# Banded and causal attention on one Trainium2 core: one ring of eight PSUM banks, results of two rows, rows 0 and 1 as one piece, triangles cut in SBUF, engines from a table, and a new order

## The chip, the core and the metric

The kernel runs on one core of one Trainium2 chip. The metric is device time in microseconds for one launch, the median of several runs. The engines are TensorE (PE; its weight loads PEld), VectorE (DVE), ScalarE (ACT), GpSimd (POOL) and SyncE (SP), whose queue issues every DMA of this kernel.

## What is computed

Two layers in a row, all in float32, for 4 batches and 768 positions. First, banded attention with sinks: 8 heads of 64, each position sees its own 128 last positions and the first 4 (the sinks). Its output, 512 wide, is the input of the second layer: 4 experts, each one head of causal attention, with the two best experts of each position kept and weighed.

```python
# first layer, scale = 1/8
keep = is_sink | ((rel >= 0) & (rel < 128))          # rel = query - key
a = softmax(where(keep, scale * q @ k.T, -1e9));  x = a @ v
# second layer
logits = x @ w_gate;  w = softmax over the top 2 of 4
for e in range(4):
    q, k, v = x @ wq[e], x @ wk[e], x @ wv[e]
    a = softmax(where(causal, -1e9, scale * q @ k.T))
    out += (w of e, where chosen) * (a @ v @ wo[e])
```

## The kernel before

**The work.** A unit of the first layer (`first`, `band_rows`) is one batch and a pair of heads: 16 units. One of the second layer (`second`, `wide_rows`) is one batch and a pair of experts: 8 units. A row is a block of 128 positions; each has six. A unit turns q and k around (transposes on PE through an identity for batch 0, on DVE for the others), multiplies them to scores, takes the minimum and the exponential, scales by the reciprocal sum, transposes the probabilities and multiplies them with the values. The second layer also projects x to q, k and v (`second`, `values`) and stores (`store`). Some rows of the second layer send their probabilities through DRAM and back in place of the transposes (`by_way_of_dram`: POOL scales, DVE transposes in blocks, SP sends `there` and back).

**In the first layer**, rows 0 and 1 are done each for itself (`edge_row`), rows 2 and 3 and rows 4 and 5 as bands of two (`both_rows`, `transposed_band`). A band takes 132 keys per query, since the upper triangle of the row's own block and the lower triangle of the block before fill one 128 wide block (`pick`). After the transposes, PSUM is copied to SBUF (`pt`), and a second copy, multiplied by the triangle `own`, is taken from PSUM by DVE (`tri`, line 1471); the weighted sum (`av`) uses both, one with the values and one with the differences of neighbouring values (`dv`).

**On PE** matmuls use the array in three shapes, which the profile prints as rows*columns: 64*128, two heads beside each other in the rows (scores, transposes, the sums over the sinks in line 1393); 128*64, two heads beside each other in the columns (weighted sums, line 1389); 128*128 (projections, gate, output). PSUM has eight banks: six tiles `b` for everything and two tiles `acc` for the weighted sums of up to four rows (`Acc`), which ACT and DVE then split into a high and a low part (`finisher`, `split`, lines 1228 and 1233).

**The order.** Every piece of work is a `Step` with a priority, the engines that can do it, a cost for each, and the buffers it needs. `Plan.emit` runs through time: of all steps that can go, it takes on each engine the one with the best priority, start time and shape of the array, with `HURRY`, `STAY` and `BULK` as weights, and `NUDGE` adds a number to the priority of single steps. The steps are then issued in that order. While PE would be idle in the first part, `fill` puts dummy products there (lines 1059 and 1062). Steps that two engines can do (copies from PSUM, `evacuate`) go to the one that is free first. Buffers of a kind form a ring and are waited for.

**Weights** come on SP's queue, wv and the gate, wq, wk and wo, through the tiles `v2` and `o`; ACT rounds them to the high part and POOL takes the difference as the low part (`weight`, lines 1186 and 1190).

Of the kernel before, what the change touches and what calls it, by code (L numbers as in the profile page):

```python
# [34 lines left out]
PSUM = ("b", "acc")  # L35

NUDGE = {
    "busy_PE": -21.445, " ": -65.5699, " busy_PE": 26.9069, " busy_PE 0": 94.2732, "sink_values_DVE": -57.9649,
    " sink_values_DVE": -0.2231, " sink_values_DVE 0": -114.2035, "load_SP": 1.3276, " load_SP": 86.4402,
    " load_SP 0": -217.458, "again_SP": -58.9971, " again_SP 0": -60.4741, "sink_values_ACT": 63.7817,  # L40
    " sink_values_ACT": 11.9388, " sink_values_ACT 0": -13.5634, "sink_values_POOL": 86.9205, " sink_values_POOL": -18.6515,
    " sink_values_POOL 0": -126.024, "sink_values_SP": 5.8101, " sink_values_SP 0": 30.073, " load_SP 1": 1.7522,
    "weight_ACT": 29.2113, " weight_ACT": 38.9392, " weight_ACT 0": 363.4815, "weight_POOL": 62.3002,
    " weight_POOL": -88.56, " weight_POOL 0": 327.5217, " weight_ACT 1": 373.0797, " weight_POOL 1": 63.7488,
# [1896 lines left out]
```

## Time and profile before

| | |
|---|---|
| median of 3 runs | 383.38 us (382.5 to 384.05) |
| profiled execution | 383.73 us, span 381.7 us |
| PE busy | 373.7 us (98%), 4116 matmul records |
| weight loads busy | 314.7 us (82%) |
| DVE, ACT, POOL busy | 317.9 (83%), 253.7 (66%), 230.2 (60%) us |
| moved by DMA | 48.06 MB, mean 126 GB/s |

The span goes from the first to the last instruction of the profiled execution. Busy times of PE include the time in which one matmul follows another late without a gap being drawn, so its share alone doesn't say how dense PE's work is; the starts of neighbouring blocks of matmuls do.

### The profile page before, as it was taken

The page shows a single profiled execution, that of the slowest core. Times are in us where ns is not written, and L with a number is a line of the kernel's source. Part 1 is how long each engine was busy: PE and PEld are TensorE (multiplying, and loading weights), DVE is VectorE, ACT ScalarE, POOL GpSimd, SP SyncE. Part 2 cuts the span into 40 slices and gives each one's busy share as a digit, 9 for nine tenths or more (in the row PEclk, how much of TensorE's full clock was granted, in tenths as well). Part 3 has the DMA queues.
Part 4 walks back from the last instruction along what each step waited for, and adds up shares of the span by engine and source line. Part 5 has one row for each costly group of instructions (what it writes and reads, how often), then busy time and mean ns, then how long its engine had stood idle before and what let it go on. Part 6 is the DMA issues. An engine that isn't in the chain of part 4 may idle for free.

```text
span 381.7 us, 12237 instructions
## 1 busy us (share of the span) xinstructions
PE 373.7 (98%) x4116; PEld 314.7 (82%) x4116; DVE 317.9 (83%) x1420; ACT 253.7 (66%) x923; POOL 230.2 (60%) x429
## 2 busy tenths in 40 slices
PE   8999999999998999999999999999999999999996
PEld 7777787988787888988888788988788888988884
DVE  7999999599998999969699999657999858447952
ACT  3898997267897578738498767514899847215921
POOL 5789997548676853356478845059187830049830
PEclk9999999999999999999999999999999999999999
DMA  7989999435676877148665894037700000012004
GB/s 161 198 188 167 180 184 179 67 61 166 198 158 160 230 179 146 23 122 283 199 141 90 224 252 102 0 113 256 234 23 3 2 2 3 29 56 84 4 2 165
DMA packets 145631, 48.06 MB, mean 126 GB/s; under 512 B 122976, under 2 KB 138336, under 8 KB 145568
## 3 DMA queue, kind: packets, MB, share of 16 engines
q1 hardware_dynamic: 145568, 47.28, 50.9%
q8 instruction: 32, 0.52, 0.6%
q14 instruction: 31, 0.25, 0.2%
HBM read 30.88 MB, written 16.12 MB: 123 GB/s over the span
## 4 chain that ended last, share of the span: by engine, by line
PE 90%; DVE 5%; DMA 1%; SPq 1%; issue 1%; ACT 0%; POOL 0%; DVEq 0%; POOLq 0%
PE acc L1389 20%; PE b L1759 18%; PE b L1358 11%; PE b L1416 10%; PE b L1786 9%; PE b L1833 9%; PE b L1363 9%; PE acc L1393 2%; PE b L1844 1%; DMA kn<-in_k_dram 1%; SPq L1507 1%; DVE p L1663 1%; DVE b L1660 1%; DMA p<-there 1%; SPq L1727 0%
## 5 line engine op out<-in xcount | busy, mean ns | idle before, releaser
L1566 ACT ACTIVATE p<-p,st 128x768 f32<-128x768 f32 (+5 forms) x96 | 63.9, 668 | 14.9 <-DVE st L1558 14.0
L1245 ACT ACTIVATE pt<-b 128x256 f32<-128x256 f32 (+2 forms) x153 | 52.0, 372 | 9.6 <-PE b L1416 8.7
L1358 PE MATMUL b<-kx,qn 64*128 64x260 f32 (+1 forms) x384 | 57.2, 390 | 0.4 <-ACT qn L1245 0.3
L1667 ACT ACTIVATE p<-p,st 128x132 f32<-128x132 f32 x128 | 50.8, 399 | 8.4 <-DVE st L1663 6.9
L1578 POOL TENSOR_TENSOR p<-p,st 128x128 f32<-128x128 f32 (+5 forms) x66 | 50.4, 787 | 1.2 <-PE b L1416 0.2
L1558 DVE CUSTOM_DVE_ANT_0 p<-b,cmask 128x384 f32<-128x384 f32 (+3 forms) x96 | 45.7, 504 | 2.9 <-PE b L1363 2.3
L1363 PE MATMUL b<-ks,qs 64*128 64x384 f32 (+3 forms) x384 | 43.5, 342 | 0.0
L1416 PE MATMUL b<-ident,p 64*128 64x64 f32 x820 | 43.2, 228 | 0.2 <-ACT kx L1245 0.2
L1641 POOL TENSOR_TENSOR p<-p,st 128x256 f32<-128x256 f32 (+1 forms) x32 | 26.6, 833 | 27.1 <-DVE st L1405 6.4
L1358 PEld LDWEIGHTS b<-kx,qn 64*128 64x128 f32 x384 | 36.6, 186 | 7.5 <-DVE st L1663 1.5
L1416 PEld LDWEIGHTS b<-ident,p 64*128 64x128 f32 x820 | 34.6, 138 | 8.8 <-issue 4.0
L1389 PE MATMUL acc<-pt,vn 128*64 128x128 f32 x448 | 40.0, 282 | 0.2
L1502 POOL TENSOR_TENSOR p<-p,st 128x640 f32<-128x640 f32 (+2 forms) x30 | 37.3, 1254 | 0.8 <-POOL st L1408 0.3
L1786 PE MATMUL b<-wvh,x 128*128 128x260 f32 x192 | 37.1, 284 | 0.0
L1363 PEld LDWEIGHTS b<-ks,qs 64*128 64x128 f32 x384 | 31.5, 186 | 3.8 <-issue 1.8
L1833 PE MATMUL b<-woh,y 128*128 128x512 f32 x96 | 33.7, 399 | 0.0
L1663 DVE CUSTOM_DVE_ANT_0 p<-b,pair_mask 128x132 f32<-128x132 f32 x128 | 33.5, 284 | 0.0
L1686 POOL TENSOR_TENSOR p<-p,st 128x512 f32<-128x512 f32 x32 | 33.1, 1041 | 0.0
L1759 PE MATMUL b<-x,wqh 128*128 128x512 f32 (+1 forms) x128 | 33.0, 343 | 0.0
L1660 DVE COPY_PREDICATED b<-earlier,b 128x128 f32<-128x128 int32 x128 | 32.3, 286 | 0.8 <-PE b L1358 0.8
L1759 PE MATMUL b<-x,wkh 128*128 128x512 f32 (+1 forms) x128 | 32.9, 343 | 0.0
L1808 POOL TENSOR_TENSOR gate<-gate 128x24 f32<-128x24 f32 x4 | 0.9, 237 | 51.8 <-DVE gate L1803 51.8
(131 smaller groups left out, 979.1 us busy)
## 6 DMA issues: line engine op xcount, KB each, us to landing
vn<-in_v_dram SPq DMA_DIRECT2D x32, 192.0 KB, 3.5
out_dram<-o SPq DMA_DIRECT2D x24, 256.0 KB, 2.0
qn<-in_q_dram SPq DMA_DIRECT2D x52, 96.0 KB, 2.5
kn<-in_k_dram SPq DMA_DIRECT2D x52, 96.0 KB, 2.5
there<-p SPq DMA_DIRECT2D x10, 384.0 KB, 3.0
p<-there SPq DMA_DIRECT2D x40, 96.0 KB, 3.3
there<-p SPq DMA_DIRECT2D x10, 320.0 KB, 2.2
p<-there SPq DMA_DIRECT2D x40, 80.0 KB, 2.3
```

The costliest lines, as they stand in the source:

```text
L1245: nc.scalar.activation(dst(), src(), AF.Copy)
L1358: nc.tensor.matmul(o, self.q_of()[hs, qs], self.ks.t[hs, 0, ks], start=True, stop=True)
L1363: nc.tensor.matmul(o, self.qs.t[hs, a, qs], self.ks.t[hs, b, ks], start=n == 0, stop=n == 2)
L1389: nc.tensor.matmul(o[e * 64:e * 64 + 64], lhs, rhs, start=e not in self.begun, stop=last and self.done == len(self.steps))
L1416: nc.tensor.transpose(t[g].t[:, n, :], x[gs], ident[gs, gs])
L1558: nc.vector.tensor_tensor_reduce(out=one(e)[:, cs], in0=s2[e].t[:, :(c1 - c0) * 128], in1=mask(c0, c1), scale=times, scalar=st.t[:, 3, es] ...
L1566: nc.scalar.activation(x, x, AF.Exp, bias=st.t[:, 0, es], scale=-1.0, accum_out=st.t[:, 1, es])
L1578: nc.gpsimd.tensor_mul(x, x, st.t[:, 2, e:e + 1].to_broadcast([128, n * 128]))
L1667: nc.scalar.activation(p.t[:, n, :], p.t[:, n, :], AF.Exp, bias=st.t[:, 0, n:n + 1], scale=-1.0, accum_out=st.t[:, 1, n:n + 1])
L1759: nc.tensor.matmul(t.t, w[a][:, c, es], X[b, c].t[:, x, cs], start=c == 0 and m == 0, stop=c == NCH - 1 and m == 2)
L1786: nc.tensor.matmul(t.t[:, :VW], X[b, c].t[:, a, qs], W["wv"][w][:, c, :], start=c == 0 and n == 0, stop=c == NCH - 1 and n == 2)
L1833: nc.tensor.matmul(t.t, Y[b, c].t[:, a, qs], W["wo"][w][:, c, :], start=c == 0 and n == 0, stop=c == EP - 1 and n == 2)
```

## The change

- `PSUM` and `kinds`: the two `acc` tiles go, and `b` has eight tiles; a weighted sum takes a bank of the same ring. Results are finished in groups of two rows (`ROWS = "0 2 4 6"`); projections keep groups of four and two (`CUTS`).
- `edge_rows` in place of `edge_row`: rows 0 and 1 have one pair of score tiles (128 and 256 columns, without the sink columns), one set of sums and reciprocals, one block of 12 transposes and one weighted sum.
- `transposed_band`: the triangle is cut from the copy in SBUF, after both copies, in one instruction of 512 columns on POOL or DVE; the weighted sum waits for it too.
- `ONLY`, a table of steps and engines: it sets which engine does a step that two can do. New such steps are the scalings (`scaled`: POOL or ACT; a band's: POOL or DVE), the low parts of the weights (`either`), the differences of values and the triangle.
- wq and wk go through the tiles `o` in two pieces each.
- `NUDGE`, `HURRY`, `STAY` and `BULK` have other numbers: the order of all engines is new.

```diff
-PSUM = ("b", "acc")
+PSUM = ("b",)
 NUDGE = {
-    "busy_PE": -21.445, " ": -65.5699, " busy_PE": 26.9069, " busy_PE 0": 94.2732, "sink_values_DVE": -57.9649,
+    "busy_PE": -150.4, " ": -5.3, " busy_PE 0": 186.9, "sink_values_DVE": -89.8, " sink_values_DVE": -42.0,
...
+ONLY = {
+    " low_POOLDVE 0": DVE, " low_POOLDVE 1": POOL, " low_POOLDVE 2": POOL, " low_POOLDVE 5": POOL, " low_POOLDVE 6": POOL,
...
-HURRY = 37.208573
-STAY = 45.808617
-BULK = -17.350682
+HURRY = 55.95
+STAY = 129.39
+BULK = -27.41
...
             s.prio += sum(NUDGE.get(name, 0.0) for name in s.part)
+            if s.part[-1] in ONLY:
+                s.cost = {ONLY[s.part[-1]]: s.cost[ONLY[s.part[-1]]]}
...
-             "b": (6, 512, F32), "acc": (2, 512, F32)}
+             "b": (8, 512, F32)}
...
-        whole = cols if tag == "v2" else n
+        whole = 512 if tag == "o" else cols
...
-                W_READY[name].append(plan.step(
-                    prio + 3, {POOL: 695},
...
+                W_READY[name].append(either(
+                    prio + 3, {POOL: 695, DVE: 335},
...
+    def scaled(prio, dst, src, n, by, after, new, use, dims=None):
+        def norm():
+            if s.eng == ACT:
+                nc.scalar.activation(dst(), src(), AF.Copy, scale=by())
+            else:
+                f = by()[:, :, None, None] if dims else by()
+                nc.gpsimd.tensor_mul(dst(), src(), f.to_broadcast(dims or [128, n]))
+        s = plan.step(prio, {POOL: pool_cost(n), ACT: 187 + 0.833 * n}, norm, after, new, use)
+        return s
...
-            self.b = buf("acc", 512)
+            self.b = buf("b", (hi - lo) * 128)
...
-            def tri(g=g, gs=gs):
-                nc.vector.tensor_mul(pt.t[:, 4:, gs], t[g].t[:, :4, :], own[:, None, gs].to_broadcast([128, 4, 64]))
...
-            moved.append(plan.step(prio, {DVE: 65 + 1.04 * 256}, tri, [tt], (), [t[g], pt]))
...
+        def tri():
+            e = nc.vector if below_own.eng == DVE else nc.gpsimd
+            e.tensor_mul(pt.t[:, 4:, :], pt.t[:, :4, :], own[:, None, :].to_broadcast([128, 4, 128]))
+        below_own = plan.step(prio, {DVE: 65 + 1.04 * 512, POOL: pool_cost(512)}, tri, moved, (), [pt])
...
-        acc.steps.append(plan.step(prio + AV_LAG, {PE: 872}, av, moved + value[1](None) + diff[1], new,
+        acc.steps.append(plan.step(prio + AV_LAG, {PE: 872}, av, [*moved, below_own] + value[1](None) + diff[1], new,
...
-            if i < 2:
-                edge_row(prio_of(i), acc, i, pair, value)
-            elif i % 2 == 0:
+            if i == 0:
+                edge_rows(prio_of(i), acc, pair, value)
+            elif i > 1 and i % 2 == 0:
...
+        st, p, sums, s2 = buf("st", 5, 4), buf("p", 768), [], two(512)
+        at = ((0, 128), (128, 384))
...
+        def both():
+            for r, (a, z) in enumerate(at):
+                pair.scores([x.t[:, a:z].rearrange("p (j c) -> p j c", c=128) for x in s2], r, range(r + 1))
...
+        tt = plan.step(prio, {PE: 4 + 61 * 6}, tr, normed, [*t, pt], [p], mode="ROWS")
...
+        def all_of():
+            acc.done += 1
+            for m, (i, j) in enumerate(((0, 0), (1, 0), (1, 1))):
+                for e in range(2):
+                    acc.add(i, e, value[0](j, e), pt.t[:, 2 * m + e, :], m == 2)
...
-        nm = plan.step(prio - LEAD_N, {POOL: pool_cost(512)}, norm, [r, kept], (), [p, st])
+        nm = plan.step(prio - LEAD_N, {POOL: pool_cost(512), DVE: 4 * 128}, norm, [r, kept], (), [p, st])
...
+    ROWS = "0 2 4 6"
...
-            weight(name, E * D, expert_pieces(src), WP + WS * n)
+            weight(name, E * D, expert_pieces(src), WP + WS * n, "o")
```

What the new numbers do is seen in the order of the instructions on an engine, at three places. The first is PE near the end of a pair of first-layer units: `pt` and `p` are probabilities, `vn` and `dv` values and their differences, `kx` and `qn` keys and queries, `sk` and `vs` the sinks; 64x128 are weighted sums, which use the array as 128*64, and all others here use it as 64*128. Before:

```order
L1389 MATMUL acc_134<-pt_105,dv_100 64x128 x2
L1358 MATMUL b_130<-kx_82,qn_66 128x260
L1358 MATMUL b_132<-kx_82,qn_66 128x260
L1393 MATMUL acc_133<-sk_113,vs_115 128x128 x2
L1393 MATMUL acc_134<-sk_112,vs_115 128x128 x2
L1389 MATMUL acc_133<-pt_106,vn_71 64x128 x2
L1389 MATMUL acc_133<-pt_106,dv_100 64x128 x2
```

After, at a place with the same kinds of steps:

```order
L1404 MATMUL b_133<-ident,p_94 128x64
L1404 MATMUL b_128<-ident,p_94 128x64
L1381 MATMUL b_132<-sk_113,vs_114 128x128 x2
L1377 MATMUL b_130<-pt_105,vn_72 64x128 x6
L1377 MATMUL b_132<-pt_107,vn_71 64x128 x2
L1377 MATMUL b_132<-pt_107,dv_100 64x128 x2
```

Before, the sums of one band stand between scores, and the shape changes there and back for each; after, the sums of rows 0 and 1 of one unit (six products, one step) and those of a band of another stand in one block. Over the whole order, neighbouring matmuls differ in shape 189 times before and 139 times after.

The second place is the triangle. On DVE before, `b` being the bank with the transposes:

```order
L1510 STREAM_TRANSPOSE p_89<-p_89 128x640
L1471 TENSOR_TENSOR pt_105<-b_127,own 128x4x64
L1404 TENSOR_REDUCE st_124<-st_124 128x2
L1405 RECIPROCAL st_124<-st_124 128x2
L1558 ISA p_92,st_126<-b_131,cmask 128x256
```

On POOL after:

```order
L1832 TENSOR_TENSOR gate_118<-gates_120 128x24
L1833 TENSOR_TENSOR gate_118<-gate_118,below 128x24
L1462 TENSOR_TENSOR pt_106<-pt_106,own 128x512
L1462 TENSOR_TENSOR pt_107<-pt_107,own 128x512
L1579 TENSOR_TENSOR vs_114<-vp,gsel 48x256
```

Two products of DVE per band with a PSUM operand became one of 512 columns, on POOL for 23 bands of 32 and on DVE for 9; it reads what the copies wrote.

The third is SP's queue where the weights come, before:

```order
L1727 DMA kn_68<-in_k_dram 32x24x32 x4
L1180 DMA v_0_83<-in_moe_wk_dram 128x4x64 x4
L1727 DMA qn_67<-in_q_dram 32x24x32 x4
L1723 DMA vn_70<-in_v_dram 128x6x64 x2
L1727 DMA kn_69<-in_k_dram 32x24x32 x4
L1727 DMA qn_65<-in_q_dram 32x24x32 x4
L1180 DMA v_0_83<-in_moe_wq_dram 128x4x64 x4
```

and after:

```order
L1747 DMA kn_68<-in_k_dram 32x24x32 x4
L1154 DMA o_117<-in_moe_wk_dram 128x2x64 x4
L1154 DMA v_0_83<-in_moe_wv_dram 128x4x64 x4
L1154 DMA v_0_83<-in_moe_w_gate_dram 128x4x4
L1747 DMA kn_69<-in_k_dram 32x24x32 x4
L1743 DMA vn_70<-in_v_dram 128x6x64 x2
L1154 DMA o_116<-in_moe_wq_dram 128x2x64 x4
```

wv now comes before wq, and wq and wk as two pieces of four DMAs each, in the two tiles `o`; the second piece of wq is the 81st DMA of the queue, where wq ended with the 66th.

## Rows read from the trace of the kernel before

**Rows 1.** The page, parts 1 and 2: busy time, share and instructions of each engine, then PE's busy tenths and the granted clock in 40 slices of the span.

```profile
PE 373.7 (98%) x4116; PEld 314.7 (82%) x4116; DVE 317.9 (83%) x1420; ACT 253.7 (66%) x923; POOL 230.2 (60%) x429
...
PE   8999999999998999999999999999999999999996
...
PEclk9999999999999999999999999999999999999999
```

**Rows 2.** The page, part 4: the chain that ended last, share of the span by engine.

```profile
PE 90%; DVE 5%; DMA 1%; SPq 1%; issue 1%; ACT 0%; POOL 0%; DVEq 0%; POOLq 0%
```

**Rows 3.** The waits of PE over the whole span, as waiting engine, tile and line, what ended the wait, and then total us, times and longest us; the three largest.

```profile
PE acc L1389 <- DMA p<-there: 1.2, 1, 1.2
PE b L1844 <- DVE lanes L1107: 1.1, 1, 1.1
PE b L1416 <- DMA kn<-in_k_dram: 0.5, 1, 0.5
```

**Rows 4.** The view by stretches: from and to (us of the span), length, then busy us of each engine with its instructions (x), granted clock, DMA share and GB/s; two of six stretches and the sum.

```profile
core 0: us, PE busy (x) PEld busy (x) DVE busy (x) ACT busy (x) POOL busy (x), PEclk, DMA share, GB/s
...
0.00:45.00 45.00, 42.12 (x514) 33.70 (x516) 40.60 (x235) 36.05 (x152) 35.74 (x77) 1.00 0.90 179
45.00:130.00 85.00, 83.80 (x916) 69.91 (x915) 77.39 (x342) 62.63 (x236) 61.66 (x115) 1.00 0.68 153
...
sum 382.00, PE 373.65 PEld 314.72 DVE 317.86 ACT 253.70 POOL 230.19; mean PE 62.28 PEld 52.45 DVE 52.98 ACT 42.28 POOL 38.37
```

**Rows 5.** The timeline of PE alone from 362.5 to 374.3 us: start us, us, engine, line, operation, tiles, shape (rows*columns of the array in use first), count.

```profile
362.54 0.71 PE L1416 MATMUL b<-ident,p 64*128 64x64 f32 x16
363.18 0.88 PE L1389 MATMUL acc<-pt,v 128*64 128x128 f32 x12
363.99 0.84 PE L1416 MATMUL b<-ident,p 64*128 64x64 f32 x20
364.76 2.19 PE L1389 MATMUL acc<-pt,v 128*64 128x128 f32 x36
366.87 0.96 PE L1416 MATMUL b<-ident,p 64*128 64x64 f32 x24
367.76 0.50 PE L1833 MATMUL b<-woh,y 128*128 128x512 f32 x1
...
368.80 0.39 PE L1833 MATMUL b<-wol,y 128*128 128x512 f32 x1
369.03 0.63 PE L1833 MATMUL b<-woh,y 128*128 128x512 f32 x2
369.50 0.39 PE L1833 MATMUL b<-wol,y 128*128 128x512 f32 x1
...
372.29 0.40 PE L1833 MATMUL b<-wol,y 128*128 128x512 f32 x1
372.52 0.40 PE L1833 MATMUL b<-woh,y 128*128 128x512 f32 x1
372.85 1.53 PE L1389 MATMUL acc<-pt,v 128*64 128x128 f32 x24
```

**Rows 6.** Groups of PE by line and form: busy us, mean ns of one, idle before.

```profile
L1358 PE MATMUL b<-kx,qn 64*128 64x260 f32 x320 | 51.3, 409 | 0.4 <-ACT qn L1245 0.3
```

**Rows 7.** Groups of DVE by line and form: count, busy us, mean ns of one, idle before it.

```profile
L1471 DVE TENSOR_TENSOR pt<-b,own 128x256 f32<-128x256 f32 x64 | 25.4, 411 | 0.1
...
L1405 DVE RECIPROCAL st<-st 128x2 f32<-128x2 f32 x80 | 13.3, 166 | 2.7
L1404 DVE TENSOR_REDUCE st<-st 128x2 f32<-128x4 f32 x80 | 11.7, 146 | 3.6 <-ACT p L1566 2.8 <-POOL psk L1681 0.3 <-ACT p L1634 0.3
L1233 DVE SCALAR_TENSOR_TENSOR x<-acc,x 128x512 fp32r<-128x512 f32 x16 | 10.9, 682 | 0.1
...
L1233 DVE SCALAR_TENSOR_TENSOR x<-acc,x 128x256 fp32r<-128x256 f32 x16 | 6.6, 411 | 0.1
L1405 DVE RECIPROCAL st<-st 128x4 f32<-128x4 f32 x32 | 5.7, 178 | 1.1
...
L1090 DVE MEMSET nought<- 128x128 f32 x1 | 0.2, 165 | 0.9 <-PEq L1924 0.9
```

**Rows 8.** Groups of ACT by line and form, in the same columns.

```profile
L1245 ACT ACTIVATE pt<-b 128x256 f32<-128x256 f32 x98 | 34.7, 378 | 5.8 <-PE b L1416 5.1 <-DVE pt L1471 0.5
...
L1566 ACT ACTIVATE p<-p,st 128x512 f32<-128x512 f32 x16 | 11.5, 724 | 5.3 <-DVE st L1558 5.2
...
L1228 ACT ACTIVATE x<-acc 128x512 fp32r<-128x512 f32 x16 | 9.4, 589 | 1.1 <-PE acc L1389 0.7 <-PE acc L1393 0.3
...
L1228 ACT ACTIVATE x<-acc 128x256 fp32r<-128x256 f32 x16 | 6.0, 378 | 0.6 <-PE acc L1389 0.6
```

**Rows 9.** Groups of POOL by line and form, in the same columns.

```profile
L1686 POOL TENSOR_TENSOR p<-p,st 128x512 f32<-128x512 f32 x32 | 33.1, 1041 | 0.0
L1603 POOL TENSOR_TENSOR dv<-vn 128x256 f32<-128x256 f32 x32 | 22.9, 732 | 3.3 <-DMA vn<-in_v_dram 2.7 <-PE acc L1389 0.3
```

**Rows 10.** When the weights come: the DMAs of wq in the timeline of SP's queue, ACT's first rounding of wq in its timeline, and from the view of line 1759 the first and last start of the matmuls that read wq.

```profile
44.77 2.09 SPq L1180 DMA_DIRECT2D v<-in_moe_wq_dram  x4
...
49.88 1.33 ACT L1186 ACTIVATE wqh<-v 128x260 fp32r<-128x260 f32 x4
...
L1759 PE MATMUL b<-x,wqh x128: 277/388/505, 59.0 to 344.4; 128*128 128x512 f32 x64, 128*128 128x256 f32 x64
```

More of the change, by code (lines that the diff above doesn't have):

```diff
@@ L1162, with either, low @@
             nc.vector.memset(t.bitcast(F32), 0.0)
+    def either(prio, cost, fn, after, new, use):
+        def low():
+            fn(nc.vector if s.eng == DVE else nc.gpsimd)
+        s = plan.step(prio, cost, low, after, new, use)
+        return s
     W, W_READY = {}, {}
@@ new lines, in edge_rows, with low, exp, norm @@
+    def edge_rows(prio, acc, pair, value):
+        st, p, sums, s2 = buf("st", 5, 4), buf("p", 768), [], two(512)
[3 more added lines that the diff above has]
+                pair.scores([x.t[:, a:z].rearrange("p (j c) -> p j c", c=128) for x in s2], r, range(r + 1))
+        mm = plan.step(prio - LEAD_S, {PE: score_cost(128, pair.exact) + score_cost(256, pair.exact)}, both,
+                       pair.inputs(0, (0, 1)) + pair.inputs(1, ()), [*s2, p, st], [pair.qs, pair.ks], fifo="s", mode="rows")
+        part = lambda r, e: p.t[:, 256 * r + e * (128 + 128 * r):][:, :128 + 128 * r]
+        for r, (a, z) in enumerate(at):
+            for e in range(2):
+                n = 2 * r + e
+                def low(r=r, e=e, n=n, a=a, z=z):
+                    nc.vector.tensor_tensor_reduce(out=part(r, e), in0=s2[e].t[:, a:z], in1=edge_mask[:, a:z], scale=-scale,
+                                                   scalar=BIG, op0=OP.add, op1=OP.min, accum_out=st.t[:, 0, n:n + 1])
+                def exp(r=r, e=e, n=n):
+                    x = part(r, e)
+                    nc.scalar.activation(x, x, AF.Exp, bias=st.t[:, 0, n:n + 1], scale=-1.0, accum_out=st.t[:, 1, n:n + 1])
+                lw = plan.step(prio - LEAD_S, {DVE: 78 + 1.04 * (z - a)}, low, [mm], (), [s2[e], p, st])
+                sums.append(plan.step(prio - LEAD_E, {ACT: 278 + 0.833 * (z - a)}, exp, [lw], (), [p, st]))
+        f = factor(prio - LEAD_N, st, sums, w=4)
+        normed = []
+        for r, (a, z) in enumerate(at):
+            def norm(r=r, a=a, z=z):
+                n = z - a
+                if made[r].eng == ACT:
+                    for e in range(2):
+                        nc.scalar.activation(part(r, e), part(r, e), AF.Copy, scale=st.t[:, 2, 2 * r + e:2 * r + e + 1])
+                else:
+                    x = p.t[:, 256 * r:256 * r + 2 * n].rearrange("p (e c) -> p e c", e=2)
+                    nc.gpsimd.tensor_mul(x, x, st.t[:, 2, 2 * r:2 * r + 2, None].to_broadcast([128, 2, n]))
+            normed.append(plan.step(prio - LEAD_N, {POOL: pool_cost(2 * (z - a)), ACT: 2 * (187 + 0.833 * (z - a))}, norm, [f], (), [p, st]))
+        made = normed
+        t, pt = two(8, 64), buf("pt", 8, 128)
+        def tr():
+            for m in range(6):
+                turned(t, m, p.t[:, (0, 128, 256, 512, 384, 640)[m]:][:, :128])
+        tt = plan.step(prio, {PE: 4 + 61 * 6}, tr, normed, [*t, pt], [p], mode="ROWS")
+        moved = [evacuate(prio, lambda g=g: pt.t[:, :6, 64 * g:64 * g + 64], lambda g=g: t[g].t[:, :6, :], 384, [tt], [t[g], pt])
+                 for g in range(2)]
+        def all_of():
+            acc.done += 1
+            for m, (i, j) in enumerate(((0, 0), (1, 0), (1, 1))):
+                for e in range(2):
+                    acc.add(i, e, value[0](j, e), pt.t[:, 2 * m + e, :], m == 2)
+        new, used = acc.bufs()
+        acc.steps.append(plan.step(prio + AV_LAG, {PE: 109 * 6}, all_of, moved + value[1]((0, 1)), new,
+                                   [pt] + value[2] + used, fifo="av", mode="cols"))
@@ L1898 @@
             f = firsts.index(u)
-            first(b, n, cuts, at_row(b, n, 0, 10.0), place[u] - (PREP_1 if b else PREP_0),
+            first(b, n, rows, at_row(b, n, 0, 10.0), place[u] - (PREP_1 if b else PREP_0),
                   -100.0 if f == 0 else place[u] - LOAD_0 if b == 0 else place[firsts[f - 1]] - PREP_1)
@@ L1904 @@
                 values(b, [(0, NB)], lambda i: at_row(b, 0, 1, 20.0)(i) - (VALUES if b else VALUES_0))
[L1905 removed]
+            second(b, n, cuts, rows, row, lambda i: at_row(b, n, 1, 0.0)(i) - (PREP_2 if b else PREP_3))
             if n == EP - 1:
```

188 lines of the change are left out of this document (126 added, 62 removed), and 1449 rows, old and new, of the table NUDGE.

## The prediction

> **What bounds the kernel now.** I read the page's busy line first. PE is busy for 373.7 of 381.7 us and no other engine for more than 83% [rows 1]; the busy tenths show it at 8 or 9 in every slice but the last, and the granted clock stands at full speed, 2.4 GHz, in every slice, so no part of the span is a clock that could rise. The chain that ended last is PE for 90% [rows 2]. Then I asked what PE waits for: the longest waits are one of 1.2 us for a DMA that brings back transposed probabilities, 1.1 us before the first instruction, and 0.5 us for the first loads of a unit [rows 3]. By stretches, PE is idle for 45.00 - 42.12 = 2.9 us in the first 45 us, for 1.2 us in the next 85, and for the other 4.0 of 8.1 us in all that follows, the end included [rows 4]. So only what makes PE's own sequence shorter shortens the kernel; work taken off DVE, ACT or POOL is worth something only where it ends one of these small waits.
>
> A busy PE is not a PE that streams columns all the time, so I looked at how its matmuls follow each other [rows 5]. The program uses the array in three shapes: 64 rows by 128 columns (scores and transposes), 128 by 64 (the weighted sums of values) and 128 by 128 (projections). In that timeline 12 records of sums (two for each product in fp32) take 363.99 - 363.18 = 0.81 us to the start of the next block and 36 take 366.87 - 364.76 = 2.11 us. That is 1.30 / 24 = 0.054 us for each record, and 0.81 - 12 x 0.054 = **0.16 us left over** in either block, whatever its length: the price of leaving that shape. For transposes, 16 take 0.64 us and 20 take 0.77 us to the next sum, so 0.0325 each and **0.12 us** for leaving; the block of 24 that goes to 128 by 128 takes 0.89 us, which gives 0.11 us at the same 0.0325 and up to 0.17 us at the 0.030 that its difference from the block of 20 gives. For projections, the 15 from 368.80 to 372.29 take 3.49 us, 0.233 each; the whole block of 21 (three between 368.80 and 369.50, and so on) takes 372.85 - 367.76 = 5.09 us, **0.20 us** more than 21 of these. PE is drawn as busy in nearly all of that time, so the busy share hides it.
>
> **The change part by part.**
>
> *The order on PE.* The amount of matrix work is the same: 3180 matmul instructions stand in the order before and 3178 in the new one, and by shape they differ only in two dummy products and in the scores of row 1. What differs is how often the shape changes. I counted it in the two orders: PE leaves 128 by 64 79 times before and 60 times now, 64 by 128 92 and 65 times, 128 by 128 18 and 14 times; 189 changes become 139. Sums of several units now stand together, and rows 0 and 1 bring one sum in place of parts. At the prices above this is 19 x 0.16 + 27 x 0.12 + 4 x 0.20 = 3.0 + 3.2 + 0.8 = **7.0 us less**, all on the path, since PE has next to no idle time in which it could be hidden. With 0.17 for the transposes it would be 8.4 us.
>
> *Rows 0 and 1 as one piece.* In 16 units two score products shrink from 260 to 256 columns. 320 records of that form take 51.3 us [rows 6], 0.16 us each; 64 records lose 4 of 260 columns: 64 x 0.16 x 4/260 = 0.16 us at most, **0.1 us** taken. The four maxima, exponentials and one set of reciprocals stand in place of two sets; row 0 now waits for row 1. That lies beside PE, as long as other matmuls are there.
>
> *Eight banks in one ring, results of two rows.* No instruction is added on PE. The 24 finishes of 512 columns and 24 of 256 become 72 of 256: on DVE 72 x 0.411 against 24 x (0.682 + 0.411), 3.4 us more [rows 7], and on ACT 72 x 0.378 against 24 x (0.589 + 0.378), 4.0 us more [rows 8], none on PE's path. A sum that is two rows long lets its results go earlier, and a bank that no sum holds can take transposes. Of the waits that this may end I see little in the rows, so it counts as nothing.
>
> *Triangles from SBUF.* 64 products of DVE from PSUM, 0.411 each, go: -26.3 us on DVE [rows 7]. In their place 23 products of 512 columns on POOL, 1.041 each, 23.9 us [rows 9], and 9 on DVE, by its 512-column row 0.68 each, 6.1 us. The weighted sum must now wait for transposes, a copy, and then the triangle, so its chain is longer by one POOL instruction, 1.04 us. What hides it is the PE work between a band's transposes and its sum. In the new order the closest pair I found has 8 other sums (16 records), 12 transposes, two small sums and three changes of shape in between: 0.87 + 0.39 + some 0.2 + 0.40 = 1.9 us, against a copy of 0.41 and the triangle's 1.04, which leaves 0.4 for handing over. If that cover were gone, each of the 32 bands would cost up to 1 us.
>
> *Engines by a table.* 75 scalings with 25,728 columns go from POOL to ACT and 32 of 128 columns to DVE. POOL: 29,800 columns at 1.041/512 leave, -60.6 us; ten differences of weights and values go too, 7.3 us by the 0.732 of [rows 9]. With the triangles POOL falls from 230 to about 186. ACT has no scaling to read a price from; its copies give 0.167 + 0.00082 a column (0.378 at 256, 0.589 at 512), its exponentials 0.30 + 0.00082 (0.724 at 512) [rows 8], so 34 to 44 us: ACT goes from 254 to between 292 and 302. I take the upper end, since the exponential also reads SBUF and a scale. DVE gets 32 scalings, between 0 and 0.411 each (nothing of that size in SBUF stands there), ten differences at 0.411, loses 32 pairs of narrow sums and reciprocals (0.166 + 0.146) and gets 16 wide ones: -10.0 + 5.2 + 4.1 + up to 13. With the triangles and finishes it comes to 300 to 313. So all three stay under PE, at some 80, 82 and 50% of 376 us, and this part costs and gains nothing but for one thing: with POOL less loaded, the probabilities sent by way of DRAM start earlier. Of the one 1.2 us wait on that way [rows 3] I take half, **0.6 us**; the bounds are 0 and 1.2.
>
> *Weights.* wq and wk come in two pieces of four DMAs each, and wv goes before wq. This is a late step to watch. Four such DMAs hold SP's queue for 2.09 us, 0.52 each [rows 10]. Before, wq's last DMA is the 66th of the queue and its block starts on PE at 59.0 us, 480 matmuls in; now it is the 81st. Fifteen more at 0.52 put it 7.8 us later, its issue ends near 54.7, and with the 3.0 us from there to ACT (49.88 - 46.86) and 2 us of rounding and differences it is ready near 60. The first product with wq is now the 499th, at the pace of before (59.0 / 480) near 61.4. It fits, with little to spare; I count nothing and give it a rival.
>
> **The sum** is made against the profiled execution, 383.73 us, of which 381.7 is the span and 2.0 lies around it: 383.73 - 7.0 - 0.1 - 0.6 = **376.0 us**. The median of the runs is 383.38, 0.35 lower, which I leave as error of the forecast.
>
> **The rivals.** *More goes than the changes of shape.* Transposes may be worth 8.4 in place of 7.0, the DMA wait its whole 1.2, and of the other waits at the start (2.9 us in the first 45, 1.1 of it before the first instruction) 1.8 may go: 383.73 - 8.4 - 0.1 - 1.2 - 1.8 = 372.2. For it speaks the free choice among eight banks; against, that the new order holds as many dummy products of half size (44) as the old, which stand where the order foresaw an idle PE.
>
> *Weights late.* If wq lands after 61.4, PE stands still once, up to 2 us: 378.0.
>
> *The freed time turns into waits.* The order may be denser than DVE and ACT can follow, and what the changes of shape gave is then spent on copies and banks that are not ready: about 383.0. For it speaks DVE's 77.4 of 85 us in the second stretch [rows 4]; against, that DVE's sum falls and that PE idles so little now.
>
> *DVE is held up by POOL.* This one ends slower. 51 instructions of DVE (9 triangles, 32 scalings, 10 differences) now have both inputs, or a plain scaled copy, in SBUF, where POOL works too; before, the triangle read PSUM. Should such an instruction wait for a running POOL instruction, that is 60% of the time [rows 1] half of 1.04 us: 51 x 0.6 x 0.52 = 16 us of lateness on DVE, and if PE had to follow all of it, 376.0 + 16 = 392. It decides the sign once more than 9 us of it reach PE, that is when DVE in some stretch becomes longer than PE. Against: DVE has 60 us to spare over the span, and POOL loses a fifth of its work. The Trainium skill states such a rule in SBUF — State Buffer, Who interferes with whom: a VectorE instruction with two SBUF inputs, or in a two-port mode, and a GpSimd instruction that reads SBUF exclude each other, and the second to start is blocked until the first ends. By that rule the 392 is the most it can come to, and no row of before shows such a pair, since every large two-operand instruction of DVE there has one input in PSUM.
>
> **How the numbers follow.** The forecast, 374 to 379, gets 0.72; more gained 0.08; weights late by enough to matter 0.08; waits in place of changes 0.07; DVE held up 0.05. The range goes from 372.0 (the second case) to 380.0 (late weights and 2 us of new waits) and leaves out the last two cases and a little. A measurement of this kernel can tell about 0.5%, 1.9 us, from no change: faster 0.88, the same 0.07, slower 0.05.
>
> **What would show it right or wrong.** Right: PE still busy for 97% or more, with about 7 us less of it; blocks of sums that still show 0.054 each and 0.16 on leaving; POOL near 186 and ACT near 300. The wait for probabilities shorter than 1.2 us or gone confirms that term. Wrong: PE idle in waits for triangles (the product with the mask, now on POOL), for wq near 60 us, or for copies by DVE; triangles on DVE that last clearly longer than 0.68; or a price per change of shape that differs from these three.

## The result, and the profile after

The changed kernel takes **385.90 us** (median of 6 runs, 385.19 to 387.61) against 383.72 of the kernel before in the same runs: a ratio of 1.0069, 95% interval 1.0047 to 1.009, so 1.8 to 3.5 us slower. The forecast was 376.0, with a range of 372.0 to 380.0. The profiled execution took 385.19 us, 9.2 more than the sum.

The page of the changed kernel, parts 1, 2 and 4 (busy time; PE's tenths and granted clock in 40 slices; the chain that ended last), beside [rows 1, 2]:

```profile
PE 367.9 (96%) x4112; PEld 315.0 (82%) x4112; DVE 319.0 (83%) x1402; ACT 286.0 (75%) x985; POOL 198.0 (52%) x374
...
PE   8999799999989899999999999999998999999996
...
PEclk9999999999989999999999999999999999999999
...
PE 70%; DVE 14%; ACT 5%; POOL 4%; DMA 3%; issue 2%; SPq 1%; DVEq 0%; ACTq 0%; POOLq 0%
```

PE's busy time fell from 373.7 to 367.9 us, nearly as forecast (366.6). But the span is 383.5: PE is idle for 15.6 us, where it was idle for 8.1 before and for 376.0 - 2.0 - 366.6 = 7.4 by the forecast. The chain tells it in one number: PE's share fell from 90% to 70%, and DVE has 14%. The granted clock, at 9 in every slice before, has an 8 in the twelfth (105.5 to 115 us). POOL came to 198.0 us where 186 was forecast, ACT to 286.0 (292 to 302), DVE to 319.0 (300 to 313).

The same stretches as in [rows 4] (columns as there):

```profile
0.00:45.00 45.00, 40.08 (x508) 32.31 (x508) 41.65 (x218) 35.86 (x150) 31.62 (x67) 1.00 0.87 180
45.00:130.00 85.00, 82.25 (x932) 71.14 (x932) 81.04 (x364) 67.89 (x246) 60.81 (x107) 0.98 0.67 146
130.00:200.00 70.00, 67.88 (x690) 58.95 (x692) 62.06 (x259) 51.59 (x178) 30.31 (x63) 1.00 0.65 169
...
270.00:340.00 70.00, 68.01 (x821) 59.62 (x818) 52.25 (x248) 52.59 (x179) 25.64 (x48) 1.00 0.14 40
```

The idle time is spread: 4.9 us in the first stretch, 2.8 in the second, 2.1 and 2.0 in the others shown, and the clock is below full speed in the second. The waits of PE (tile and line; what ended the wait; total us, times, longest), beside [rows 3]:

```profile
PE b L1404 <- DVE x L1207: 1.8, 3, 1.0
PE b L1779 <- DVE st L1545: 1.7, 1, 1.7
PE b L1377 <- DVE pt L1462: 1.3, 2, 1.1
...
PE b L1346 <- DVE st L1623: 1.0, 2, 0.8
PE b L1404 <- POOL p L1641: 1.0, 1, 1.0
```

The wait for probabilities by way of DRAM is gone, as hoped. In its place PE waits for DVE, in four of these five (the line left out is the wait ahead of the first instruction, which stood there before). Groups of DVE and POOL by line and form (count, busy us, mean ns of one, idle before) say why; the second row is from the view of line 1704 alone (shortest, median and longest in ns):

```profile
L1704 DVE TENSOR_SCALAR p<-p,st 128x128 f32<-128x128 f32 x32 | 14.7, 522 | 0.0
L1704 DVE TENSOR_SCALAR p<-p,st x32: 247/275/2926, 13.0 to 293.8; 128x128 f32<-128x128 f32 x32
...
L1462 DVE TENSOR_TENSOR pt<-pt,own 128x512 f32<-128x512 f32 x9 | 7.3, 810 | 0.0
...
L1588 DVE TENSOR_TENSOR dv<-vn 128x256 f32<-128x256 f32 x2 | 2.7, 1397 | 0.0
```

```profile
L1462 POOL TENSOR_TENSOR pt<-pt,own 128x512 f32<-128x512 f32 x23 | 29.6, 1291 | 19.7 <-ACT pt L1219 14.1 <-DVE sk L1221 4.1 <-DVE pt L1221 0.8
```

The scalings have a mean of 522 ns, more than the 0.411 us that the sum took as their upper end; that mean hides undisturbed ones of 0.25 to 0.28 and one of 2.93. Triangles on DVE take 0.81 in the mean where 0.68 was taken, the pair of differences 1.4 each. On POOL a triangle takes 1.29 where 1.04 was taken. One place shows in full how the time is lost. DVE, POOL and PE in their timelines near 105 us (start, length, instruction, count, idle before):

```profile
104.28 2.46 DVE L1704 TENSOR_SCALAR p<-p,st 128x128 f32<-128x128 f32 x4
106.67 0.41 DVE L1207 SCALAR_TENSOR_TENSOR x<-b,x 128x256 fp32r<-128x256 f32 x1
...
107.61 0.07 DVE L1679 DVE_READ_ACCUMULATOR2_ANT st<- 128x1 f32 x1
...
109.32 0.07 DVE L1623 DVE_READ_ACCUMULATOR2_ANT st<- 128x1 f32 x1
```

```profile
104.05 1.42 POOL L1588 TENSOR_TENSOR dv<-vn 128x256 f32<-128x256 f32 x2
105.43 1.04 POOL L1641 TENSOR_TENSOR p<-p,st 128x512 f32<-128x512 f32 x1
```

```profile
103.83 0.61 PE L1377 MATMUL b<-pt,v 128*64 128x128 f32 x8
104.26 2.57 PE L1377 MATMUL b<-p,v 128*64 128x128 f32 x44
106.77 0.64 PE L1404 MATMUL b<-ident,p 64*128 64x64 f32 x13
107.74 0.46 PE L1404 MATMUL b<-ident,p 64*128 64x64 f32 x7 [0.33 <-DVE st L1679]
...
109.45 1.52 PE L1346 MATMUL b<-kx,qn 64*128 64x260 f32 x5 [0.79 <-DVE st L1623]
```

Four scalings that take 1.0 us undisturbed last 2.46, until POOL has ended three instructions in a row (104.05 to 106.47). What stands behind them in DVE's queue is 1.5 us late, and PE waits twice, 0.33 and 0.79 us, for the instructions of lines 1679 and 1623 in that queue. A third loss follows (the view by stretches, columns as above):

```profile
105.00:108.00 3.00, 2.67 (x55) 2.37 (x51) 3.00 (x11) 1.46 (x7) 1.47 (x2) 1.00 0.65 135
108.00:111.00 3.00, 2.21 (x17) 1.76 (x13) 2.96 (x15) 3.00 (x13) 0.64 (x4) 0.81 0.64 171
111.00:114.00 3.00, 3.00 (x31) 2.60 (x30) 2.58 (x16) 1.77 (x7) 1.77 (x3) 0.62 0.76 134
```

PE was busy for 2.67 of the 3 us from 105 and for 2.21 of the 3 from 108, and its granted clock went to the lower level, 1.2 GHz, for part of the stretches from 108 and from 111: a mean of 0.81 and of 0.62 is 2 x 0.19 x 3 + 2 x 0.38 x 3 = 3.4 us at half speed, 1.7 us lost. Not every wait costs the clock: around PE's longest, 1.7 us at 132.5, it stayed at 1.00.

Instruction by instruction, 20 of DVE's (scalings, triangles, differences of values and of weights) lasted 13.2 us longer than their undisturbed length, each with a POOL instruction over it; 8 us of that are scalings. The stalls of PE that follow within a few us are 1.7 near 41 us, 1.3 near 108, 1.7 at 132.5, 0.2 near 199 and 1.8 near 290: 6.7 us (the expectations below take them as 7.3). That this is their cause was a reading; the experiments test it.

### The profile page after: what moved, and what is told of

The parts are those of the page before. It is cut to its first block, busy times and chain, and to the rows that moved or that the text cites. A ratio compares the mean times of both kernels' runs of the same rounds, so it can differ in the third digit from the quotient of the medians.

```text
span 383.5 us, 12160 instructions
## 1 busy us (share of the span) xinstructions
PE 367.9 (96%) x4112; PEld 315.0 (82%) x4112; DVE 319.0 (83%) x1402; ACT 286.0 (75%) x985; POOL 198.0 (52%) x374
## 4 chain that ended last, share of the span: by engine, by line
PE 70%; DVE 14%; ACT 5%; POOL 4%; DMA 3%; issue 2%; SPq 1%; DVEq 0%; ACTq 0%; POOLq 0%
PE b L1779 18%; PE b L1377 13%; PE b L1853 9%; PE b L1806 8%; PE b L1346 7%; PE b L1351 7%; PE b L1404 6%; DVE p L1704 2%; DVE b L1676 2%; POOL pt L1462 2%; DVE p L1623 2%; DVE p L1679 2%; DVE p L1545 1%; ACT p L1683 1%; DMA there<-p 1%
## 5 line engine op out<-in xcount | busy, mean ns | idle before, releaser
L1553 ACT ACTIVATE p<-p,st 128x512 f32<-128x512 f32 (+5 forms) x96 | 63.7, 667 | 7.3 <-DVE st L1545 7.0
L1346 PE MATMUL b<-kx,qn 64*128 64x260 f32 (+2 forms) x384 | 54.4, 385 | 2.5 <-DVE st L1623 1.0
L1219 ACT ACTIVATE pt<-b 128x384 f32<-128x384 f32 (+3 forms) x122 | 46.3, 421 | 6.6 <-PE b L1404 5.1
L1231 POOL TENSOR_TENSOR p<-p,st 128x640 f32<-128x640 f32 (+5 forms) x51 | 47.9, 954 | 1.6
L1404 PE MATMUL b<-ident,p 64*128 64x64 f32 x820 | 39.7, 226 | 1.7 <-POOL p L1641 1.0
L1377 PE MATMUL b<-pt,vn 128*64 128x128 f32 x448 | 39.6, 280 | 0.3 <-ACT pt L1219 0.3
L1462 POOL TENSOR_TENSOR pt<-pt,own 128x512 f32<-128x512 f32 x23 | 29.6, 1291 | 19.7 <-ACT pt L1219 14.1
L1806 PEld LDWEIGHTS b<-wvh,x 128*128 128x128 f32 x192 | 30.3, 188 | 1.1 <-DVE st L1679 0.3
L1628 ACT ACTIVATE p<-p,st 128x128 f32<-128x128 f32 (+1 forms) x64 | 28.7, 450 | 2.6 <-DVE st L1623 2.3
L1377 PEld LDWEIGHTS b<-pt,vn 128*64 128x64 f32 x448 | 25.6, 136 | 4.1 <-issue 1.0
```

The lines of the kernel that those rows point to most:

```text
L1219: nc.scalar.activation(dst(), src(), AF.Copy)
L1231: nc.gpsimd.tensor_mul(dst(), src(), f.to_broadcast(dims or [128, n]))
L1346: nc.tensor.matmul(o, self.q_of()[hs, qs], keys(hs, 0), start=True, stop=True)
L1377: nc.tensor.matmul(o[e * 64:e * 64 + 64], lhs, rhs, start=e not in self.begun, stop=last and self.done == len(self.steps))
L1404: nc.tensor.transpose(t[g].t[:, n, :], x[gs], ident[gs, gs])
L1553: nc.scalar.activation(x, x, AF.Exp, bias=st.t[:, 0, es], scale=-1.0, accum_out=st.t[:, 1, es])
```

## The experiments

All keep the order of instructions on PE. The engine that a step uses is overruled after the order is made, where the loop calls it (`s.fn()`). The expectations give their rival explanations letters: B, certain kinds of DVE instruction are held up by POOL; L, DVE is simply too full; D, the new order leaves too little room between a result and its use; S, O and W are explained where they come up.

**What holds up what.** A kernel of single instructions, each kind alone and beside five products of POOL.

> This kernel leaves the whole attention out. It times single instructions of VectorE in SBUF and PSUM, each kind first alone and then with five products of GpSimd (128x512, both inputs in SBUF, 1.04 us each in the changed kernel) beside it. Theory B (a VectorE instruction that scales within SBUF, or has two inputs there, is blocked while GpSimd works in SBUF): scalings of 128 columns alone 0.25 us each, beside GpSimd the first ones wait for a whole product or several, so that the row of 12 takes over 5 us in place of 3; products of two SBUF inputs (0.68 alone) likewise; products with one input in PSUM, transposes and copies out of PSUM the same in both stretches (0.41, 0.56, 0.41); ScalarE's scalings the same. Theory L (VectorE was simply too full, the long instructions are an artefact of it): every kind takes the same time in both stretches, within 10%. GpSimd's product with a repeated 128-column operand: 1.29 us, with a repeated column 1.04.

DVE's timeline, for each kind first alone, then beside POOL (L40 scalings, L44 products of two SBUF inputs, L48 products with one input in PSUM, L52 transposes):

```profile
5.34 2.43 DVE L40 TENSOR_SCALAR ddst<-dsrc,fac 128x128 f32<-128x128 f32 x12
...
9.13 5.57 DVE L40 TENSOR_SCALAR ddst<-dsrc,fac 128x128 f32<-128x128 f32 x12
...
15.17 4.32 DVE L44 TENSOR_TENSOR ddst<-dsrc,own 128x512 f32<-128x512 f32 x6
...
20.85 7.18 DVE L44 TENSOR_TENSOR ddst<-dsrc,own 128x512 f32<-128x512 f32 x6
...
28.50 4.54 DVE L48 TENSOR_TENSOR ddst<-ps,own 128x256 f32<-128x256 f32 x10
...
34.40 4.54 DVE L48 TENSOR_TENSOR ddst<-ps,own 128x256 f32<-128x256 f32 x10
...
39.41 4.86 DVE L52 STREAM_TRANSPOSE ddst<-dsrc 128x384 f32<-128x384 f32 x8
...
45.59 4.85 DVE L52 STREAM_TRANSPOSE ddst<-dsrc 128x384 f32<-128x384 f32 x8
```

Scalings and products of two SBUF inputs are held up (2.43 to 5.57, 4.32 to 7.18); the others are not, to 0.01 us, and neither are copies out of PSUM (4.54 in both). Theory B holds for the kinds that the change brought in, and the kinds tried that stood there before are free of it: the old triangle read PSUM.

**All of it to POOL.**

```
-            s.fn()
+            s.eng = POOL if s.eng == DVE and s.part and "POOL" in s.part[0] else s.eng; s.fn()
```

> The order on TensorE and ScalarE is kept; the 8 times 4 scalings, the 9 triangles, 8 differences of weights and one pair of differences of values that VectorE took go to GpSimd, which then has about 28 us more. Theory B: 20 of these instructions were late by 13.2 us in all, and stalls of TensorE of 7.3 us followed them (1.7 near 41 us, 1.3 near 108, 1.8 at 132.5, 0.3 near 199, 2.2 near 290), with 1.7 us of half clock behind the second; most of it goes, and GpSimd's own queue gives 1 to 3 us of new waits: 377 to 382. Theory L (VectorE too full): the same direction, since 24 us of work leave VectorE. Theory D (the new order itself leaves too little room between a result and its use): 384 to 387.

387.47 us (386.89 to 388.63), ratio 1.0107 [1.0083, 1.0131]: above the range of every theory. PE's longest waits, and its second stretch:

```profile
PE b L1377 <- POOL pt L1462: 2.6, 3, 1.4
PE b L1381 <- POOL vs L1579: 2.2, 2, 2.0
```

```profile
45.00:130.00 85.00, 82.60 (x918) 72.25 (x920) 71.98 (x338) 65.07 (x235) 65.08 (x113) 0.94 0.65 141
```

The long waits for DVE went, but 20 us more on POOL (218.2 in all) made others for POOL, and a mean clock of 0.94 is 2 x 0.06 x 85 = 10 us at half speed. It says nothing on theory D, since it brought a cost of its own.

**Scalings to ACT, differences of values to POOL; and the same with DVE kept as full.**

```
-            s.fn()
+            s.eng = {"norm_POOLDVE": ACT, "differences_POOLDVE": POOL}.get(s.part[0], s.eng) if s.eng == DVE and s.part else s.eng; s.fn()
...
-                    nc.vector.tensor_scalar(p.t[:, n, :128], ...)
+                    nc.vector.tensor_scalar(p.t[:, n, :128], ...) if nm.eng == DVE else nc.scalar.activation(p.t[:, n, :128], p.t[:, n, :128], AF.Copy, scale=f()[:, n:n + 1])
```

> The order on TensorE is kept; the 8 times 4 scalings go from VectorE to ScalarE (about 9.6 us more there) and the one pair of differences of values to GpSimd. Triangles and weights stay on VectorE. Theory B: stalls of 7.0 of 7.3 us lose their cause, the half clock near 111 us goes: 377 to 379.5, granted clock 1.00. Theory L: 380 to 384, since only 11 us of VectorE's 319 leave. Theory D: 384 to 387.

> As the one before, but where VectorE had a scaling it now transposes a spare tile of 128x128 in SBUF (some 0.25 us, its result is used by nobody), and two of 128x256 where it had the differences, so that VectorE's queue is as full as in the changed kernel and only the kind of instruction differs. Theory B: within 1.5 us of the kernel without these transposes, 377 to 381. Theory L: as the changed kernel, 384 to 387. Theory D: 384 to 387.

381.25 us (ratio 0.9934 [0.9914, 0.9953]) and 381.26 (0.9953 [0.9933, 0.9974]). The first number lies in theory L's range too (380 to 384), so the second kernel has to decide. Its busy times show a DVE as full as in the changed kernel, less time in which it was held up (6.6 us less):

```profile
PE 366.7 (97%) x4112; PEld 314.3 (83%) x4112; DVE 312.4 (82%) x1403; ACT 294.5 (78%) x1017; POOL 199.1 (52%) x376
```

So it is the kind of instruction and not the load: theory L, with 384 to 387 for this kernel, falls. Theory D falls for 4.6 us. The first was to give 377 to 379.5 and is 1.8 above that, the second 0.3 above its 381. The first kernel's ACT and PE near 16 us show what the move cost:

```profile
14.53 1.26 ACT L1704 ACTIVATE p<-p,st 128x128 f32<-128x128 f32 x4
15.70 0.47 ACT L1219 ACTIVATE pt<-b 128x384 f32<-128x384 f32 x1
```

```profile
16.32 0.40 PE L1404 MATMUL b<-ident,psk 64*128 64x64 f32 x2 [1.06 <-ACT pt L1219]
```

Four scalings, 1.26 us, now stand ahead of a copy in ACT's queue, and PE waits 1.06 us for the copy. The 12 executions of the second kernel also give a price for the clock: at a mean granted clock of 1.000 they took 380.6 to 381.1 us, at 0.991 383.3 to 383.6, so 2.5 us for 0.009. The six of the changed kernel stand at 0.986 to 0.995, those of the kernel before at 0.998 to 1.000.

**Where the scalings cost least.** First with the first step left on DVE, then with no scalings at all, then with no triangles either.

```
+ ... and s.part[-1][:3] != "000"           (first step stays on DVE)
-                for n in range(4):         (no scalings; differences on POOL)
+                for n in range(0):
-            e.tensor_mul(pt.t[:, 4:, :], pt.t[:, :4, :], own[...])     (and no triangles)
+            return
```

> As the kernel with scalings on ScalarE and differences on GpSimd (381.25 us), but the first of the 8 steps, near 14 us, stays on VectorE, where it had not been late (0.3 us each). Theory S (the moved scalings make the new stalls: on ScalarE's queue four of them, 1.26 us, stand ahead of the copy of transposes for which TensorE waits 1.1 us at 16.3): 380.2, give or take 0.5, the stall at 16.3 gone. Theory O (that wait belongs to the order and has another cause): 381.2.

> The four scalings of each of the 8 steps are left out (those probabilities stay unnormalised, nobody does the work); the differences of values are on GpSimd. The rest is the changed kernel, in its order. It shows what the order gives if these 32 instructions cost nothing. Theory S: against the kernel with scalings on ScalarE the stalls of 1.1 at 16.3, 0.9 at 194.8, 0.7 at 290.1 and half of the 1.0 at 109 go too: 377.5 to 378.8. Theory O (the rest of the distance to 376.0 lies in the order): 380.5 to 381.5.

> As the one before, and all 32 triangles are left out too (the weighted sum reads the copied half in their place): 29.6 us less on GpSimd, 7.3 on VectorE. If the longer chain by way of the triangle still costs: its waits were 0.4, 0.3, 0.3, 0.2 us and smaller ones, so 1.0 to 1.5 us less than without scalings. If GpSimd's queue behind the triangles costs as well (waits for its scalings of rows 0 and 1, 0.8 at 46.7, 0.4 at 55): up to 2.5 less. If what hides the triangles is enough: the same within 0.5.

380.22 us (0.9928 [0.9906, 0.995]) as theory S had it, and the wait at 16.3 us is gone from the trace; by the ratios the gain is 0.2 us, within the intervals. Without scalings **376.61** (0.9833 [0.981, 0.9857]), below what was expected: nearly the whole distance from 385.9 to the forecast hangs on 32 small instructions and one pair of differences. That counts the scalings' own work too, which this kernel leaves out. Without triangles too, 372.99 (0.9736 [0.9711, 0.9762]), 3.6 us less, more than the 2.5 expected at most: the triangles are not hidden.

**Another kind at the same places; differences alone.**

```
-                    nc.vector.tensor_scalar(p.t[:, n, :128], p.t[:, n, :128], f()[:, n:n + 1], None, op0=OP.mult)
+                    nc.vector.transpose(p.t[:, n, :128], p.t[:, n, :128])
```

> Each of the 32 scalings that VectorE did becomes a transpose of 32x32 blocks of the same tile in place (those probabilities stay unnormalised and turned): the same number of instructions at the same places, with the same waits before and behind, 0.34 us from one to the next in the kernel with transposes of a spare tile, so a little longer than a scaling that nothing holds up. The differences of values are on GpSimd. Theory B (it is the kind of instruction that is held up by GpSimd): near the kernel without scalings, 377 to 379. Theory W (any four more instructions in that chain and on VectorE's queue do it): 383 to 385.

> Only the one pair of differences of values of the third image goes from VectorE to GpSimd; the scalings stay on VectorE. Theory B: the stall of 1.8 us at 132.5 behind it goes, and nothing else: 383.5 to 384.5. Theory W: the time that TensorE stood there comes up again in the next wait: 385 to 386.

378.61 us (0.9864 [0.984, 0.9888]) with the transposes, 7.3 us less than the changed kernel: the same queue, the same places, and an instruction as long as an undisturbed scaling (0.20 us from one to the next, not the 0.34 expected). Shortest, median and longest of the 32, in ns:

```profile
L1704 DVE STREAM_TRANSPOSE p<-p x32: 268/271/309, 13.2 to 287.4; 128x128 f32<-128x128 f32 x32
```

The differences alone gave 385.25 (1.0039 [1.0023, 1.0055]). Both kernels have the differences on POOL and were timed in the same rounds, so they differ in the kind of these 32 instructions and in nothing else: 6.6 us. Theory W, with 383 to 385 for the first, falls. What the differences gain alone is 0.65 us by the medians and 1.2 by the ratios, whose intervals overlap, where 1.4 to 2.4 was expected. That number lies in the range of theory W (385 to 386), but no other wait of PE grew. The stretches of the second kernel:

```profile
45.00:130.00 85.00, 83.31 (x952) 72.29 (x950) 80.53 (x363) 67.52 (x245) 60.27 (x106) 0.97 0.66 142
130.00:200.00 70.00, 69.59 (x722) 60.55 (x720) 61.86 (x270) 53.63 (x187) 33.44 (x67) 1.00 0.66 172
```

From 130 to 200 us PE is busy 1.7 us more, so the stall is gone; the clock ahead of it is lower than in the changed kernel's profile (0.97 against 0.98). What the differences cost by themselves is between 0.65 and 1.7 us, and stays open.

**Which form is not held up.**

> This kernel leaves the whole attention out. Four ways to scale 128 columns in SBUF on VectorE, each alone and then with five products of GpSimd (128x512) beside it: the scaling of the changed kernel (0.20 us from one to the next alone, 0.46 beside GpSimd in the first series of this kind); 129 columns read as 3 rows of 43 that touch; 129 columns read as 3 rows of 43 out of 44; and 128 columns with the sum written out as well. If what holds it up is that a plain scaled copy uses both of VectorE's ways into SBUF, the third and fourth take 0.32 to 0.45 alone and the same beside GpSimd; if any work within SBUF is held up, all four are about twice as long beside GpSimd. GpSimd's cut of a triangle by an index, 4 times 128 columns with one input, against its product with a mask, 1.26: if the second input sets the price, 0.5 to 0.9; if not, 1.1 to 1.4.

DVE's timeline (L40 the plain scaling, L48 3 rows of 43 out of 44; alone, then beside POOL), the view of line 52 (the scaling that also writes its sum, in both stretches: shortest, median and longest in ns) and two groups of POOL:

```profile
5.41 3.83 DVE L40 TENSOR_SCALAR ddst<-dsrc,fac 128x128 f32<-128x128 f32 x12
...
10.60 6.87 DVE L40 TENSOR_SCALAR ddst<-dsrc,fac 128x128 f32<-128x128 f32 x12
...
30.52 4.56 DVE L48 TENSOR_SCALAR ddst<-dsrc,fac 128x129 f32<-128x129 f32 x12
...
36.43 4.55 DVE L48 TENSOR_SCALAR ddst<-dsrc,fac 128x129 f32<-128x129 f32 x12
```

```profile
L52 DVE TENSOR_SCALAR_CACHE_REDUCE ddst<-dsrc,fac x24: 333/346/347, 41.5 to 51.7; 128x128 f32<-128x128 f32 x24
```

```profile
L63 POOL TENSOR_TENSOR pdst<-psrc,own 128x512 f32<-128x512 f32 x4 | 5.0, 1262 | 0.2
L60 POOL TENSOR_SCALAR_AFFINE_SELECT pdst<-psrc 128x512 f32<-128x512 f32 x4 | 2.6, 639 | 0.2
```

Rows that touch are held up like the plain scaling (3.86 us alone, 6.89 beside POOL). Rows that do not touch are free of it (4.56 and 4.55), and so is the form that also writes its sum, one every 0.39 us in either stretch. A triangle cut by an index takes 0.64 us on POOL, half the product with a mask.

**Whole kernels from this.**

```
-            s.fn()
+            s.eng = POOL if s.eng == DVE and s.part and s.part[0] in ("differences_POOLDVE", "tri_DVEPOOL") else s.eng; s.fn()
...
-                    nc.vector.tensor_scalar(..., None, op0=OP.mult)
+                    nc.vector.tensor_scalar(..., None, op0=OP.mult, op1=OP.add, accum_out=total)
...
-            e.tensor_mul(pt.t[:, 4:, :], pt.t[:, :4, :], own[:, None, :].to_broadcast([128, 4, 128]))
+            nc.gpsimd.affine_select(out=pt.t[:, 4:, :], in_=pt.t[:, :4, :], pattern=[[0, 4], [1, 128]], compare_op=OP.is_ge, fill=0.0, base=0, channel_multiplier=-1)
```

This is the first kernel; the second has the same triangles, with the scalings as in the kernel of 380.22 us.

> A whole kernel in the order of the changed one: the 32 scalings stay on VectorE in the form that also writes out its sum (0.39 us from one to the next, with or without GpSimd beside it, against 0.20 for the plain one alone), the differences of values go to GpSimd, and all 32 triangles go to GpSimd as a cut by an index (0.64 us in place of 1.29 for the product with the mask). Theory B (held-up scalings and long triangles were the loss): with turns in place of the scalings it was 378.6, the longer form adds up to 1 us, and the shorter triangles give back 1 to 3.6 us (3.6 is what leaving them out gave): 375.5 to 378.5. If the length of the triangle does not count: 378.5 to 380.

> As the kernel with 7 steps of scalings on ScalarE and the first on VectorE (380.2), and all triangles on GpSimd as a cut by an index. Theory B: 1 to 3.6 us less, 376.6 to 379.2. If the length of the triangle does not count: 379.7 to 380.7.

The first takes **378.05 us** (377.9 to 379.82; ratio 0.9854 [0.9832, 0.9877]), 5.8 less than the kernel before and 7.9 less than the changed one. Its scalings on DVE (shortest, median and longest in ns) and what is still held up there:

```profile
L1704 DVE TENSOR_SCALAR_CACHE_REDUCE p<-p,st x32: 303/346/349, 13.0 to 286.6; 128x128 f32<-128x128 f32 x32
...
L1164 DVE TENSOR_TENSOR wvl<-v,wvh 128x260 fp32r<-128x260 f32 x2 | 2.6, 1305 | 0.0
```

No scaling takes more than 0.35 us; the differences of weights, two SBUF inputs each, still wait (1.3 us where 0.42 is undisturbed). The second takes 380.79 (0.9914 [0.9892, 0.9936]), 0.6 more than the kernel with the long triangles by the medians and 0.5 less by the ratios, so not told apart from it. No triangle is left on DVE in this kernel either. So the length of the triangle on POOL, and the nine on DVE that could be held up, are not what most of the 3.6 us went to (1.7 at most by the intervals). The extra stage before the weighted sum is left; no run tests it by itself.

## Why the prediction was wrong, step by step

- **The order on PE: right.** Forecast 7.0 us less busy time, 8.4 at most. Three kernels of the same order whose clock stayed at full speed up to the end (scalings on ACT, the same with DVE kept full, no scalings) show 365.9, 366.7 and 365.2 against 373.7: 7.0 to 8.5. The one price of leaving a shape that was looked up again holds nearly: the 52 records of sums above take 106.77 - 103.83 = 2.94 us, 52 x 0.054 and 0.13 more (0.16 was taken).
- **Rows 0 and 1** (0.1 us) are too small to be told apart here. **The DMA wait: right**, all of the 1.2 is gone where half was taken. **Weights late: did not happen**; the first product with wq stands at 63.4 us and waited for nothing.
- **Triangles, counted as 0: wrong.** The cover was worked out as 1.9 us against 1.45 and handing over, with POOL's product at the 1.04 of a row whose second input is a repeated column [rows 9]. With a repeated tile it is 1.29 (1.26 alone), so 0.2 was left for handing over, and leaving the triangles out gives 3.6 us. This did not move the result away from 376.0, since the order without scalings came to 376.6 with the triangles in it: some 3 us were gained that the sum does not name, 1.4 of them in PE's busy time (365.2 where 366.6 was forecast). That the two nearly cancel is luck.
- **The engine table, "costs and gains nothing": the step that failed.** It summed engines over the span (DVE 300 to 313 of 376) and let 32 scalings cost 0 to 0.411 us each. What counts in a queue that is worked off in order is how late one of them makes the next instruction. Delays of 2.7 us (near 37 us), 1.5 (near 105) and 1.9 (near 129) were followed by stalls of PE of 1.7, 1.1 and 1.7, so the cover on PE was a microsecond or less. The kind of the 32 scalings alone is worth 6.6 us. The prediction named this as its last rival, with nearly the right size (16 us of lateness on DVE; 13.2 measured), and gave it 0.05 because DVE had 60 us to spare. That argument was the fault: of 13.2 us of lateness 6.7 came through to PE. The size is right in part by luck: it took some 31 delays of 0.52 us, and there were 20 of 0.66. Nor is its 392 the most it could come to, since 0.52 is a mean and one scaling alone was 2.7 us late. The rival's condition, a stretch in which DVE is longer than PE, was met in the first 45 us alone (41.65 against 40.08); the stalls near 290 us fell into a stretch where DVE was busy for 52 of 70. Of the signs of being wrong that the prediction listed, two came: PE idle in waits for DVE, and triangles on DVE well over 0.68 (0.81 in the mean).
- **A clock that could fall** was in no case of the prediction. The stalls cost a second time: 1.7 us in the profiled run, some 2.5 at 0.991, near which this kernel's executions stand. With 6.7 that is 8.4 to 9.2 of the 9.9 between 376.0 and 385.9. This sum is read from stalls; the 6.6 us above rest on runs alone.

The Trainium skill states the rule behind the rival in SBUF — State Buffer, Who interferes with whom: VectorE and GpSimd share a pair of SBUF ports that one holds for a whole instruction, VectorE when it has two SBUF inputs or works in a two-port mode, and a scaling that writes out its accumulator has no such mode. The runs agree on what is held up and what is not (2.43 to 5.57, 4.32 to 7.18, and 0.39 in both stretches); the ports themselves no run here shows.

## What to carry to other kernels

Work that is moved to an engine with time to spare is judged by what stands behind it in that engine's queue, not by the engine's share of the span: ask for the longest delay of one instruction and compare it with the cover of the next wait. Before work goes to VectorE within SBUF while GpSimd is busy there, choose the form: one input in PSUM, a transpose, or a scaling with its sum written out were not held up here, and a product of two SBUF tensors or a plain scaling was. Where TensorE is the bound, a stall may cost its clock as well (waits of 0.33 and 0.79 us here, and 1.7 us lost to the clock behind them), so price both.

## What the runs showed that was not expected

- A held-up VectorE instruction can wait for several of GpSimd's, not only for the one that runs: one scaling lasted 2.93 us, over four of them.
- Beside back-to-back products of GpSimd, scalings that write four places in turn go in pairs: one of 0.27 us, then one of 1.06. Where all write one place, four in a row took 0.95 to 1.08 each. Products of two inputs slow both sides (0.69 to 1.41 on VectorE, 1.04 to 1.37 on GpSimd).
- The price of a GpSimd product depends on how its second input repeats: 1.04 us for a column, 1.26 for a tile of 128, and an index cut of the same 512 columns takes 0.64.
- 12 plain scalings take 2.43 us when they read and write four places in turn and 3.83 when all read one and write one.
